# Issuing one transposing load of x from ScalarE, and the first weights all from SyncE

## The chip, the cores and the metric

The kernel runs on one core of one Trainium2 chip. The metric is the device time of one execution in microseconds (us), as the median of several runs. Beside the times there is one profiled execution: a trace with the start and duration of every instruction on every engine, and of the DMA transfers. TensorE is called PE in it (its weight loads PEld), VectorE DVE, ScalarE ACT, GpSimd POOL, SyncE SP. "SPq" and "ACTq" are the instructions of SP and ACT that issue a DMA; the 16 DMA engines of the core then move the data.

## What is computed

Two attention blocks, A and B, of the same shape, with a cache of keys and values; their outputs stand side by side. Each has its own x, k_cache, v_cache, wq and wo, all in bf16.

```python
# B, Sq, D = 16, 32, 1024;  Hq, Hkv, Sk, Dh = 32, 4, 512, 128
q = (x @ wq).reshape(B, Sq, Hq, Dh).transpose(0, 2, 1, 3)
k = jnp.repeat(k_cache, Hq // Hkv, axis=1)
v = jnp.repeat(v_cache, Hq // Hkv, axis=1)
p = softmax(einsum("bhqd,bhkd->bhqk", q, k) * Dh ** -0.5)
o = einsum("bhqk,bhkd->bhqd", p, v)
out = o.transpose(0, 2, 1, 3).reshape(B, Sq, Hq * Dh) @ wo
```

So the work for a block is a projection of 512 tokens by 1024 columns to 32 heads, the attention, and a projection back.

## The kernel before

The bulk of the kernel is one hand-ordered stream of matmuls. A loop of slots (line 613) goes over 128 pairs of a batch entry and a group of heads. In each slot PE gets four score matmuls (line 357), four value matmuls (line 425), and about seven matmuls from a stream of "units" that fill it up: the query projection of the heads still to come (line 301) and the output projections (line 320). Nothing reorders the instructions: each engine runs its own in the order in which the code emits them, and waits on semaphores where data of another engine or of a DMA is needed. DMA issues are instructions in that order too, so a DMA issue that has to wait holds up everything behind it on the same engine.

The change is in the start of the kernel, before that loop (lines 455 to 556). Here the first eight heads of block A are projected. The contraction over the 1024 columns of x goes in eight chunks of 128, called chunk 0 to 7. A matmul of chunk d and head h takes the weights `w0[d // 4][:, d % 4, h]` and the transposed x `xT[0][:, d, :]`, with 512 tokens as columns, and adds into the bank of head h. For each chunk, two things must be on the chip:

- The weights. `load_w0(d0, d1, h0, h1, eng)` loads the rows of chunks d0 to d1 for heads h0 to h1, 32 KB for a chunk and a head. Chunk 0 is loaded in two halves of three heads (96 KB each), chunks 1, 2 and 3 for six heads each (192 KB), the other two heads of chunks 0 to 3 in one transfer (256 KB), then chunk 4, chunks 5 and 6, chunk 7 for all eight heads (256 KB a chunk). In the trace these tiles are called `w_sb`, line 474.
- The transposed x. Chunks 0 and 1 are loaded as they are, in two halves of the tokens (`load_x`, line 465, 128 KB each, one half by SP and one by ACT), transposed by PE (line 521) and copied to `xT` by DVE and ACT (line 525). Chunks 2 and 3, 4 and 5, 6 and 7 are loaded by a DMA that transposes, two chunks at a time (`load_x_transposed`, line 468, 256 KB each).

PE's order there: 22 matmuls on a constant tile (`warm_up`, line 513) while the first data come; the eight transposes of x; chunk 0 of heads 0 to 2 in two halves of the tokens and of heads 3 to 5; chunks 1, 2 and 3 of heads 0 to 5; chunks 0 to 3 of heads 6 and 7; chunks 4, 5 and 6 of all heads; chunk 7 with the copy of each head to `qT` (line 553). All these matmuls have line 531. Behind them come 16 units of line 301 for heads 8 and 9, then the loop.

Order of the DMA issues before the change (SP, if nothing else is named): the second half of x by ACT; the first half of x; chunk 0 of heads 0 to 2; chunk 0 of heads 3 to 5 by ACT; chunk 1; chunk 2 by ACT; the transposing load of chunks 2 and 3; chunk 3; heads 6 and 7 of chunks 0 to 3; chunk 4; the transposing load of chunks 4 and 5; the weights of chunks 5 and 6; the transposing load of chunks 6 and 7; the weights of chunk 7. Then the weights of heads 8 to 11 in two halves (`wq_sb`, line 246), the four transposing loads of the first keys (`kT`, line 275), the weights of heads 12 to 15, the next keys, the first values (`v_sb`, line 283), and so on. ACT loads its table of functions (line 480) between its first two issues.

The DMAs of SP and ACT take their completion semaphores in turn from a set of eight, in the order of the code. An issue whose semaphore was used before waits until the DMA that used it last has completed. Before the change the transposing load of chunks 4 and 5 waits in this way for the load of chunk 0 (heads 0 to 2).

Of the kernel before, what the change touches and what calls it, by code (L numbers as in the profile page):

```python
# [181 lines left out]
def kernel(  # L182
# [14 lines left out]
    nc = tc.nc  # L197
# [20 lines left out]
    def fast_path(ok_i):  # L218
        with ExitStack() as fctx:
# [235 lines left out]
            NF = REP - 2  # L455
# [8 lines left out]
            def load_x(t0, t1, eng=nc.sync):  # L464
                eng.dma_start(out=x_sb[:, t0:t1, :], in_=x_v[:, t0:t1, 0:2 * P])  # L465

            def load_x_transposed(d0):
                nc.sync.dma_start_transpose(
                    out=xT[0][:, d0:d0 + 2, :],
                    in_=A_x.flatten_outer_dims()[:, d0 * P:(d0 + 2) * P],  # L470
                )

            def load_w0(d0, d1, h0, h1, eng=nc.sync):
                eng.dma_start(  # L474
                    out=w0[d0 // HC][:, d0 % HC:(d1 - 1) % HC + 1, h0 * DH:h1 * DH],
                    in_=wq_v[:, d0:d1, h0 * DH:h1 * DH],
                )

            load_x(TT // 2, TT, nc.scalar)
            nc.scalar.preload_act_table_set("natural_log_exp_and_others")  # L480
            load_x(0, TT // 2)
            load_w0(0, 1, 0, NF // 2)
            load_w0(0, 1, NF // 2, NF, nc.scalar)
            load_w0(1, 2, 0, NF)
            load_w0(2, 3, 0, NF, nc.scalar)
            load_x_transposed(2)
            load_w0(3, 4, 0, NF)
            load_w0(0, HC, NF, REP)
            load_w0(HC, HC + 1, 0, REP)
            load_x_transposed(HC)  # L490
            load_w0(HC + 1, DC - 1, 0, REP)
            load_x_transposed(HC + 2)
            load_w0(DC - 1, DC, 0, REP)
            load_wq(0, 2, 0, 2)
# [173 lines left out]
    ok_i = flag.tile([1, 1], I32, name="ok_i")  # L668
    total = 2 * 2 * NG * QW
    ok = fast_path(ok_i)  # L670
    with tc.If(ok < total, preferred_fallthrough_block=True, label="general"):
        general_path(tc, problems, out_flat)
# [30 lines left out]
```

## Time and profile before

| | |
|---|---|
| median of 4 runs | 343.18 us (342.87 to 343.43) |
| the profiled execution | 343.06 us |
| its span, first to last instruction | 341.2 us |
| PE busy | 337.0 us, 99% of the span |
| DVE, ACT, POOL busy | 265.4, 185.4, 47.0 us |
| DMA moved in the span | 71.70 MB, 210 GB/s on average |
| queue of SP and queue of ACT: packets | 127504 and 704 |
| granted clock of PE | 1.0 throughout |

The landing times of the first transfers, by their issues:

| transfer | issued at, by | lands after |
|---|---|---|
| x, first half | 0.74 us, SP | 2.2 us |
| x, second half | 0.82, ACT | 2.6 |
| chunk 0, heads 0 to 2 | 1.25, SP | 2.9 |
| chunk 0, heads 3 to 5 | 1.34, ACT | 3.3 |
| chunk 1 | 1.75, SP | 4.5 |
| chunk 2 | 1.83, ACT | 4.7 |
| chunks 2 and 3 of x, transposing | 2.22, SP | 5.2 |
| chunk 3 | 3.60, SP | 4.3 |
| heads 6, 7 of chunks 0 to 3 | 4.22, SP | 4.6 |
| chunk 4 | 4.69, SP | 5.0 |
| chunks 4 and 5 of x, transposing | 5.25, SP | 5.3 |

How to read it: times in the trace count from the first instruction. A line of a timeline gives start, duration, engine, line of the code, operation, the tile written and the tiles read, and how many instructions were merged into it; in brackets the idle time of that engine before it and what ended it. The chain of waits is followed back from the last instruction: at each step to what released it. The busy share of a DMA queue adds up the durations of its packets, so it can exceed 1 where an engine has packets of two queues under way.

### The profile page before, as it was taken

How to read it: one execution, taken by the hardware profiler on the slowest of the kernel's cores; microseconds unless marked ns; L12 is line 12 of the kernel's file. 1: busy time of each engine (PE TensorE's matmuls, PEld its weight loads, DVE VectorE, ACT ScalarE, POOL GpSimd, SP SyncE). 2: the span in 40 equal slices, each digit the busy share in tenths (PEclk: the TensorE clock that was granted, in tenths of full speed). 3: DMA queues.
4: the chain of work that ended last, by engine and by line, in shares of the span. 5: the costliest groups of instructions: out<-in, count | busy, mean ns of one | idle time of the engine just before them, and what ended most of it. 6: DMA issues, size and time to landing. Idle time of an engine off the chain costs nothing.

```text
span 341.2 us, 5475 instructions
## 1 busy us (share of the span) xinstructions
PE 337.0 (99%) x2113; PEld 213.2 (62%) x2113; DVE 265.4 (78%) x335; ACT 185.4 (54%) x208; POOL 47.0 (14%) x206
## 2 busy tenths in 40 slices
PE   8999999999999999999999999999999999999996
PEld 6455666666666666666666666666666666666555
DVE  0047988888988898888888988879888888889540
ACT  2058666666667667666645545555554555555110
POOL 0001110011111111110012221222122101111100
PEclk9999999999999999999999999999999999999999
DMA  8979999989999898999999965998449997440001
GB/s 200 307 186 263 291 243 222 186 226 267 308 282 154 239 223 234 205 294 303 319 294 273 254 125 146 335 284 224 111 110 292 357 188 177 98 108 12 17 19 33
DMA packets 128622, 71.70 MB, mean 210 GB/s; under 512 B 76880, under 2 KB 127824, under 8 KB 128592
## 3 DMA queue, kind: packets, MB, share of 16 engines
q1 hardware_dynamic: 127504, 69.78, 84.2%
q0 software_dynamic: 384, 1.05, 0.8%
q10 hardware_dynamic: 704, 0.49, 0.5%
q8 instruction: 17, 0.28, 0.4%
q14 instruction: 13, 0.11, 0.1%
HBM read 50.59 MB, written 2.10 MB: 154 GB/s over the span
## 4 chain that ended last, share of the span: by engine, by line
PE 97%; DMA 1%; SPq 0%; ACT 0%; issue 0%; ACTq 0%
PE f_ps L320 32%; PE q_ps L301 28%; PE s_ps L357 16%; PE ob L425 16%; PE q_ps L531 4%; DMA w_sb<-in_A_wq_dram 1%; SPq L465 0%; SPq L474 0%; ACT o_sb L329 0%; ACTq L329 0%
## 5 line engine op out<-in xcount | busy, mean ns | idle before, releaser
L365 ACT ACTIVATE p_sb<-s_ps,shift 128x1024 bf16<-128x1024 f32 x128 | 142.7, 1115 | 97.5 <-PE s_ps L357 87.0
L376 DVE TRANSPOSE_TENSOR_REDUCE parts<-p_sb 128x32 f32<-128x1024 bf16 x128 | 158.8, 1240 | 20.7 <-ACT p_sb L365 19.3
L320 PE MATMUL f_ps<-wo_sb,oT 128*128 128x512 bf16 (+1 forms) x544 | 132.3, 366 | 0.0
L301 PE MATMUL q_ps<-xT,wq_sb 128*128 128x512 bf16 x448 | 116.9, 379 | 0.0
L357 PE MATMUL s_ps<-qT,kT 128*128 128x256 bf16 x512 | 76.8, 273 | 0.0
L425 PE MATMUL ob<-p_sb,v_sb 128*128 128x256 bf16 x512 | 76.8, 273 | 0.0
L320 PEld LDWEIGHTS <-oT 128*128 128x128 bf16 x544 | 53.2, 98 | 35.3
L357 PEld LDWEIGHTS <-kT 128*128 128x128 bf16 x512 | 56.9, 113 | 28.3
L301 PEld LDWEIGHTS <-wq_sb 128*128 128x128 bf16 x448 | 43.8, 98 | 32.2
L425 PEld LDWEIGHTS <-v_sb 128*128 128x128 bf16 x512 | 50.1, 98 | 20.0
L447 DVE TENSOR_TENSOR oT<-r,ob 128x512 bf16<-128x512 f32 x64 | 43.9, 686 | 19.8 <-PE ob L425 19.4
L411 DVE STREAM_TRANSPOSE r<-rall 128x512 f32<-128x512 f32 x64 | 44.2, 691 | 1.1
L309 ACT CAST qT<-q_ps 128x512 bf16<-128x512 f32 x56 | 32.7, 583 | 16.5 <-PE q_ps L301 16.5
L394 POOL COPY half<-cs 64x32 f32<-64x32 f32 x32 | 6.6, 206 | 231.5 <-DVE cs L384 231.5
L329 ACT CAST o_sb<-f_ps 128x512 bf16<-128x512 f32 (+1 forms) x17 | 9.5, 559 | 23.6 <-PE f_ps L320 23.6
L531 PE MATMUL q_ps<-xT,w_sb 128*128 128x512 bf16 (+1 forms) x67 | 14.6, 379 | 0.2 <-DMA w_sb<-in_A_wq_dram 0.2
L406 DVE RECIPROCAL rall<-sums 128x32 f32<-128x32 f32 x32 | 10.5, 327 | 3.3 <-POOL sums L403 3.3
L384 DVE TENSOR_REDUCE cs<-parts 128x32 f32<-128x128 f32 x32 | 12.1, 377 | 1.1
L553 DVE CAST qT<-q_ps 128x512 bf16<-128x512 f32 x4 | 2.5, 682 | 13.3 <-PE q_ps L531 13.3
L531 PEld LDWEIGHTS <-w_sb 128*128 128x128 bf16 x67 | 6.6, 101 | 7.9 <-DMA w_sb<-in_A_wq_dram 0.9
L553 ACT CAST qT<-q_ps 128x512 bf16<-128x512 f32 x4 | 2.1, 599 | 12.8 <-PE q_ps L531 12.8
L331 POOL DMA_DIRECT2D out_dram<-o_sb x8 | 4.6, 575 | 29.2 <-ACT o_sb L329 29.2
(25 smaller groups left out, 48.7 us busy)
## 6 DMA issues: line engine op xcount, KB each, us to landing
v_sb<-in_A_v_cache_dram SPq DMA_DIRECT2D x16, 512.0 KB, 5.9
wq_sb<-in_B_wq_dram SPq DMA_DIRECT2D x8, 1024.0 KB, 5.8
wo_sb<-in_A_wo_dram SPq DMA_DIRECT2D x8, 1024.0 KB, 7.5
v_sb<-in_B_v_cache_dram SPq DMA_DIRECT2D x16, 512.0 KB, 5.2
wo_sb<-in_B_wo_dram SPq DMA_DIRECT2D x8, 1024.0 KB, 8.5
wq_sb<-in_A_wq_dram SPq DMA_DIRECT2D x5, 1024.0 KB, 6.6
wq_sb<-in_A_wq_dram SPq DMA_DIRECT2D x2, 512.0 KB, 7.2
kT<-in_A_k_cache_dram SPq DMA_TRANSPOSE x64, 4.4
```

Source lines behind the costliest of these rows:

```text
L301: nc.tensor.matmul(ps[:], lhsT=w[:, dc, (h % 4) * DH:(h % 4 + 1) * DH], rhs=xT[pr][:, dc, :], start=(dc == 0), stop=(dc == DC - 1),)
L309: nc.scalar.copy(out=qT[pr, g][:, :, hl, :], in_=ps[:].rearrange("p (b s) -> p b s", s=SQ),)
L320: nc.tensor.matmul(ps[:, 0:width], lhsT=oT[pr, tt][:, h, :], rhs=wo_tiles[pr, nh, h // REP][:, h % REP, off:off + width], start=(h == 0), ...
L357: nc.tensor.matmul(s_ps[:, c, :], lhsT=kT[:, i % GRP, c, :], rhs=qT[pr, g][:, b, :, :].rearrange("p h s -> p (h s)"), start=True, stop=True,)
L365: nc.scalar.activation(out=p_sb[:], in_=s_ps[:], func=ACTF.Exp, bias=shift[:], scale=SCALE)
L376: nc.vector.tensor_reduce(out=parts[k][:, q, :, :].rearrange("p c h -> p (c h)"), in_=st[i]["p"][:].rearrange("p c (h s) -> p (c h) s", s=SQ),
L384: nc.vector.tensor_reduce(out=cs[:], in_=parts.pop(k)[:].rearrange("p q c h -> p q h c"), axis=AX.X, op=ALU.add,)
L406: nc.vector.reciprocal(out=rall[:, k, :], in_=quad.pop(k)[:])
L411: nc.vector.transpose(out=r[:].rearrange("p n s -> p (n s)"), in_=rall[:, k, o * 2 * REP:(o + 1) * 2 * REP] .unsqueeze(2).to_broadcast([P, ...
L425: nc.tensor.matmul(ob[j][:, q, :], lhsT=v_sb[:, i % GRP, c, :], rhs=st[i]["p"][:, c, :], start=(c == 0), stop=(c == KC - 1),)
L447: nc.vector.tensor_tensor(out=out, in0=rcp.pop(j)[:].rearrange("p (q h) s -> p q h s", h=REP), in1=ob.pop(j)[:].rearrange("p q (h s) -> p ...
L531: nc.tensor.matmul(first_q[h][:, ts], lhsT=w0[dc // HC][:, dc % HC, h * DH:(h + 1) * DH], rhs=xT[0][:, dc, ts], start=(dc == 0 and t0 == 0 ...
```

## The change

The transposing load of chunks 2 and 3 of x is issued by ACT, after its half of x and its table load, and stands in the code ahead of all weights. The second half of chunk 0 and chunk 2 of the weights, which ACT issued, are issued by SP, in their old places. The computation is the same, and so are the instructions of PE, DVE and POOL. ACT has one DMA issue fewer, SP one fewer of the transposing kind and two more of the plain kind.

```diff
-            def load_x_transposed(d0):
-                nc.sync.dma_start_transpose(
+            def load_x_transposed(d0, eng=nc.sync):
+                eng.dma_start_transpose(
                     out=xT[0][:, d0:d0 + 2, :],
                     in_=A_x.flatten_outer_dims()[:, d0 * P:(d0 + 2) * P],
                 )
...
             load_x(TT // 2, TT, nc.scalar)
             nc.scalar.preload_act_table_set("natural_log_exp_and_others")
             load_x(0, TT // 2)
+            load_x_transposed(2, nc.scalar)
             load_w0(0, 1, 0, NF // 2)
-            load_w0(0, 1, NF // 2, NF, nc.scalar)
+            load_w0(0, 1, NF // 2, NF)
             load_w0(1, 2, 0, NF)
-            load_w0(2, 3, 0, NF, nc.scalar)
-            load_x_transposed(2)
+            load_w0(2, 3, 0, NF)
             load_w0(3, 4, 0, NF)
             load_w0(0, HC, NF, REP)
             load_w0(HC, HC + 1, 0, REP)
```

Since the order in the code has changed, so has the turn of the eight semaphores: in the built kernel the transposing load of chunks 4 and 5 on SP now waits for the completion of the transposing load of chunks 2 and 3 on ACT, and the ones behind it each for one of the loads of chunks 0 to 2. From the first `kT` on the waits are the same as before.

## Prediction

> **What bounds the kernel now.** I read the page's chain first: PE holds 97% of it and DMA 1%, so a transfer can set the time only where PE waits for it. Two pieces of the chain, in its order of time, show the one place:
>
> ```profile
> 1.75 4.53 DMA w_sb<-in_A_wq_dram
> 6.32 12.69 PE q_ps L531 x58
> ```
>
> The weights of chunk 1 (call them w1, and so on by chunk; w0a and w0b are the two halves of chunk 0) are issued at 1.75 us, land at 6.28, and release PE at 6.32. From there to the last matmul I find no gap in PE's instructions. So the change can act in two ways alone: it moves that 6.32, or it makes a new gap behind it. The timeline of PE, columns start, duration, instructions:
>
> ```profile
> 3.24 1.06 PE L521 MATMUL xT_ps<-ident,x_sb 128*128 128x128 bf16 x8
> 4.21 1.92 PE L531 MATMUL q_ps<-xT,w_sb 128*128 128x256 bf16 x9
> 6.32 12.69 PE L531 MATMUL q_ps<-xT,w_sb 128*128 128x512 bf16 x58 [0.19 <-DMA w_sb<-in_A_wq_dram]
> 18.85 3.62 PE L301 MATMUL q_ps<-xT,wq_sb 128*128 128x512 bf16 x16
> ```
>
> 58 matmuls start in 18.85 - 6.32 = 12.53 us: 0.216 us each. The ninth of the group before starts at 5.75, so PE would be free for w1 at 5.96. The bubble is 6.32 - 5.96 = 0.36 us, and that is all a faster start can win, but for some 0.1 us if w0a, which lands at 4.17 just ahead of the 4.21, came sooner. Then the queues, SP's and ACT's timelines:
>
> ```profile
> 0.74 0.45 SPq L465 DMA_DIRECT2D x_sb<-in_A_x_dram  x1
> 1.25 0.92 SPq L474 DMA_DIRECT2D w_sb<-in_A_wq_dram  x2
> 2.22 1.33 SPq L468 DMA_TRANSPOSE xT<-in_A_x_dram  x1
> 3.60 1.60 SPq L474 DMA_DIRECT2D w_sb<-in_A_wq_dram  x3
> 5.25 1.60 SPq L468 DMA_TRANSPOSE xT<-in_A_x_dram  x1
> 6.89 0.58 SPq L474 DMA_DIRECT2D w_sb<-in_A_wq_dram  x1
> 1.34 0.94 ACTq L474 DMA_DIRECT2D w_sb<-in_A_wq_dram  x2
> 3.91 0.80 ACT L525 COPY xT<-xT_ps 128x256 bf16<-128x256 bf16 x2 [1.31 <-PE xT_ps L521]
> ```
>
> The first transposing load (chunks 2 and 3, called T2; T4 and T6 follow) costs its queue 1.33 us to issue and lands 5.2 us after 2.22, at 7.43. PE wants it with chunk 2, six matmuls after 6.32, at 7.63: 0.2 us to spare. Last, the DMA engines by windows; the last two columns are their busy share and GB/s:
>
> ```profile
> 1.00:2.00 1.00, 1.00 (x11) 1.00 (x12) 0.00 (x0) 0.69 (x1) 0.32 (x2) 1.00 0.07 21
> 2.00:3.00 1.00, 1.00 (x12) 1.00 (x11) 0.00 (x0) 0.60 (x1) 0.00 (x0) 1.00 0.91 274
> 3.00:4.00 1.00, 1.00 (x13) 1.00 (x10) 0.29 (x1) 0.09 (x1) 0.00 (x0) 1.00 0.88 218
> 4.00:5.00 1.00, 1.00 (x7) 0.62 (x6) 0.29 (x1) 0.66 (x2) 0.00 (x0) 1.00 0.98 281
> 5.00:6.00 1.00, 1.00 (x7) 0.45 (x4) 0.00 (x0) 0.00 (x0) 0.00 (x0) 1.00 1.24 177
> 6.00:7.00 1.00, 0.81 (x5) 0.33 (x5) 0.00 (x0) 0.00 (x0) 0.00 (x0) 1.00 1.10 271
> 7.00:8.00 1.00, 1.00 (x6) 0.47 (x5) 0.00 (x0) 0.00 (x0) 0.00 (x0) 1.00 1.11 289
> ```
>
> They are busy from 2 us on, so bytes and their order set the landings, not the moment of issue. Two facts from the records of single packets. First, while both queues hold weights, an engine takes one packet of SP's and one of ACT's in turn; where T2 meets leftover weights the same is seen (weight packets starting at 5.526, 5.602, 5.677 us: one 61 ns weight packet and one 14 ns packet of T2 per turn). Second, T2 stops at its half: 13 packets started between 5.39 and 5.92 take 240 to 768 ns instead of 18, and all end near 6.15, when the last engine is through its weights. That is the 177 GB/s row.
>
> **The change, part by part.**
>
> *Issue.* T2 leaves SP (1.33 us) for ACT, at 1.34, where w0b and w2 were (0.45 us each). SP issues x, w0a, w0b, w1, w2, w3, the last two heads of chunks 0 to 3 (w0-3), and w4 in a row, about 0.5 us each: w0b at 1.75, w1 at 2.25, w3 at 3.25, w4 at 4.3. ACT's queue is done with T2 at 1.34 + 1.33 = 2.67, at worst 1.34 + 3.51 = 4.85 (the longest transposing issue in the trace, L275 at 11.92). Behind it stand the two copies of L525, now at 3.91, for chunk 1, which PE starts at 5.96: even 4.85 + 0.80 is in time. Cost nothing.
>
> *w0b* now lands behind x (256 KB), w0a and itself (192) and its share of T2 (16 of 64 packets an engine, 64 KB). Before, it landed at 4.64 with the first two alone, so 64 KB / 245 GB/s later (245 is 1,047 KB by 6.28, summed over the windows, in the 4.28 us from 2.0): 4.9. PE wants it at 5.32. Hidden.
>
> *w1.* Before: x 256, w0a and w0b 192, w1 and w2 in turn 384, together 832 KB to 6.28. With turns against T2: 256 + 192 + 192 + 24/64 of T2 (96) = 736 KB, 96 KB less, 0.39 us sooner: 5.9. If T2 were served whole ahead of it: 896 KB, 6.28 + 0.26 = 6.54. I take about 6.0, being nearer to the turns that the packets show: gain 0.3 us. Chunk 2 is then wanted at 6.0 + 6 x 0.216 = 7.3.
>
> *T2.* This is the term that decides. T2 has 64 packets an engine. In turns it ends beside w0a, w0b, w1, w2, w3 (8 each) and 24 of w0-3's 32: 256 + 768 + 192 + 256 = 1,472 KB. Before, its last packet left at 6.85 after 1,201 KB by the windows. 271 KB more at the 289 GB/s of the 7 to 8 row is 0.93 us: 7.78, and with the 0.58 from last packet to landing 8.36. Against that, in the 177 GB/s stretch the held engines had nothing else to move; now SP's queue has w3 and w0-3 for them. Regained: about 281 - 177 = 100 KB, 0.35 us, so 8.0. If instead T2 gets more packets a turn it ends with w2, at 1,088 KB, and lands at 7.0. The bounds are 7.0 and, with the hold felt twice (8.36 plus up to 0.75), 9.1. I take 8.0. Chunk 2 starts at 8.05, against 7.63: a loss of 0.42, the 0.3 of w1 swallowed in it.
>
> The Trainium skill speaks against the change here: "DMA: Bandwidth & Descriptors", section "Issuing engines are not separate DMA queues", says that DMAs from several engines share the same 16 DMA engines and interleave, and that issuing from more of them saves only the issue time. By that rule alone T2's landing would stay put and the sum would be the w1 term at most; the packets' turns agree with the interleaving and add that T2 loses its place.
>
> *SP behind T2.* T4's issue waits on the semaphore that T2 completes (the eight DMA semaphores go round, and T2 and T4 now share one), so at 5.25 before, at 8.0 now. That is new, and SP's queue is behind it. T4: 8.0 + 3.3 (a transposing load half its size took 2.65, L275 at 18.87, plus half of T2's 1.15 us of packets) = 11.3; at the worst 8.0 + 5.3 = 13.3, its landing time under a full queue, which there will hardly be. PE wants chunk 4 after 20 more matmuls: 8.05 + 4.31 = 12.36. Chunks 5 to 7 keep a similar margin. The DMA engines run dry for about 0.3 us before T4 and 0.6 us behind it, so what follows slides by about 1 us: the first wq_sb (lands 16.7, wanted at 18.85) and the kT of slot 0 (19.2, wanted 22.3) have more; the wq_sb for head 12 (issued 20.17, lands 25.86, wanted 27.07) has 1.2, and 1.6 once PE itself is 0.42 later. Cost nothing; without that cover, whatever exceeds 1.6 us.
>
> *Sum.* Profiled execution: 343.06 us, of which 341.2 is the span and 1.86 lies around it. 343.06 + 0.42 = 343.5. The median of the runs shown is 343.18, 0.12 above it, so 343.6.
>
> **Rivals.**
>
> *A: T2 is much later (slower).* Place: the matmuls of chunk 2. If a held transposing packet also blocks the weights behind it on its engine, nothing is regained: 8.36, plus the hold itself. It decides once T2 lands after 8.32, where the loss is 0.69. Price: 8.36 to 9.1, 0.8 to 1.5 us, typically 344.2. For: the DMA share of 1.24 beside 177 GB/s shows packets that occupy engines without moving bytes. Against: the slow engines, which set the end, are not themselves held.
>
> *B: T2 goes ahead in larger portions, or fills the pauses in the weights.* It lands by 7.3 and w1 gates alone, between 5.96 and 6.54: -0.36 to +0.22, about 343.0. For: the 13 held packets started after long unbroken runs of T2. Against: the turns of one.
>
> *C: the slide on SP comes out at PE.* T2 lands late and the 1 us grows past 1.6 us, at head 12 or the first kT: another 0.5 to 1, 344.5. For: SP is in order and its kT issues already took 8.21 us. Against: they were held by full queues, which give the delay back.
>
> *D: it does nothing.* SP stalls on T2 all the same and the bytes are the same: 343.2 within 0.1. That is the middle of B and is counted there.
>
> **How the numbers follow.** Forecast 0.40, A 0.27, B with D 0.27, C 0.06. What a measurement of this kernel can tell from no change is about 0.2%, 0.69 us. The forecast's own range is 343.3 to 343.87 and lies within it; a win above 0.69 exceeds the whole bubble, so faster gets 0.03; A and C make slower 0.32, allowing a little of A to stay under; same 0.65. The range takes in B's gain and most of A: 342.8 to 344.5.
>
> **What would show it.** In the profile after: T2's issue on ACT at about 1.34; w1 landing near 6.0 and chunk 1 starting there; a new gap of about 0.7 us before chunk 2, put down to the transposing load; SP waiting until about 8.0 ahead of T4; no gap at chunks 4 to 7 or at L301. If the gap is before chunk 1 and not before chunk 2, T2 was served first and B holds. If the first gap is after 12 us, C does. If T2 lands beyond 8.4, A. A time under 342.7 would mean that something in the start which I hold fixed, the first 4.2 us, has moved.

## The result, and the profile after

| | before | after |
|---|---|---|
| median | 343.13 us (72 runs, 342.42 to 343.68) | 343.98 us (46 runs, 343.13 to 348.85) |
| after / before | | 1.0044, 95% interval 1.0033 to 1.0056 |
| forecast | | 343.6 (342.8 to 344.5) |

The kernel became slower by 0.44%, beyond what can be told from no change. The ratio is near that of the means (344.80 / 343.09, 1.0050); the medians alone give 1.0025, because the changed kernel has something that the one before has not: executions that differ by 5.7 us among themselves, against 1.3. The profile that came with the result is of an execution at 348.60 us, among the longest. A second profile of the same kernel, run again as the first experiment, is of one at 344.33 and is read first. Both lie above the median: an execution with a smaller loss was not profiled.

PE's timeline in that second profile (start, duration; in brackets the idle time ahead and what ended it):

```profile
4.36 1.40 PE L531 MATMUL q_ps<-xT,w_sb 128*128 128x256 bf16 x6
6.92 13.34 PE L531 MATMUL q_ps<-xT,w_sb 128*128 128x512 bf16 x61 [1.16 <-DMA w_sb<-in_A_wq_dram]
20.10 3.62 PE L301 MATMUL q_ps<-xT,wq_sb 128*128 128x512 bf16 x16
```

Before, nine matmuls ran without a break from 4.21, six for heads 0 to 2 of chunk 0 and three for heads 3 to 5. Now only the first six do. The three for heads 3 to 5 stand at the head of the group that starts at 6.92, behind 1.16 us of idle time. From there no further gap appears up to line 301, which starts at 20.10 instead of 18.85. These 1.25 us are the whole loss of this execution: 344.33 - 343.06 = 1.27.

What was late is in the chain of the same profile:

```profile
1.75 5.13 DMA w_sb<-in_A_wq_dram
6.92 13.12 PE q_ps L531 x60
```

SP's issue at 1.75 is w0b. It landed at 6.88; before, issued by ACT at 1.34, it landed at 4.64. The queues of SP and ACT look as forecast:

```profile
1.25 3.66 SPq L474 DMA_DIRECT2D w_sb<-in_A_wq_dram  x7
7.10 1.34 SPq L468 DMA_TRANSPOSE xT<-in_A_x_dram  x1
```

```profile
1.34 1.33 ACTq L468 DMA_TRANSPOSE xT<-in_A_x_dram  x1
4.13 0.80 ACT L525 COPY xT<-xT_ps 128x256 bf16<-128x256 bf16 x2 [1.53 <-PE xT_ps L521]
```

T2 is issued at 1.34 in 1.33 us, the seven loads of weights in a row from 1.25, and T4 waits for T2's landing at 7.09. The windows of the DMA engines (the last two columns are their busy share and GB/s):

```profile
3.00:4.00 1.00, 0.96 (x11) 0.63 (x9) 0.08 (x1) 0.00 (x0) 0.00 (x0) 1.00 1.16 290
4.00:5.00 1.00, 1.00 (x9) 0.71 (x8) 0.50 (x2) 0.75 (x2) 0.00 (x0) 1.00 1.34 133
5.00:6.00 1.00, 0.76 (x4) 0.27 (x2) 0.00 (x0) 0.00 (x0) 0.00 (x0) 1.00 1.22 181
6.00:7.00 1.00, 0.08 (x1) 0.08 (x2) 0.00 (x0) 0.00 (x0) 0.00 (x0) 1.00 1.01 229
```

From 4 to 5 us, when w0b should come, the engines are busier than in any row shown of before (1.34, against 1.24 at most) and move 133 GB/s; before, the same row had 281. T2 and w0 are under way together there, on two queues, and that is what the row shows: packets that hold engines without moving bytes.

The long execution (348.60 us) has the same gap, longer, and one thing more. PE's timeline, then its windows (behind the window and its length PE's busy share and matmuls; third from the end the granted clock):

```profile
5.27 0.83 PE L531 MATMUL q_ps<-xT,w_sb 128*128 128x256 bf16 x6 [1.13 <-DMA w_sb<-in_A_wq_dram]
8.63 15.89 PE L531 MATMUL q_ps<-xT,w_sb 128*128 128x512 bf16 x61 [2.54 <-DMA w_sb<-in_A_wq_dram]
24.36 1.89 PE L301 MATMUL q_ps<-xT,wq_sb 128*128 128x512 bf16 x8
```

```profile
6.00:7.00 1.00, 0.10 (x1) 0.00 (x0) 0.00 (x0) 0.00 (x0) 0.00 (x0) 1.00 1.16 163
7.00:8.00 1.00, 0.00 (x0) 0.00 (x0) 0.00 (x0) 0.00 (x0) 0.00 (x0) 0.51 1.02 137
8.00:9.00 1.00, 0.36 (x1) 0.13 (x2) 0.00 (x0) 0.00 (x0) 0.00 (x0) 0.50 0.99 285
...
12.00:13.00 1.00, 1.00 (x4) 0.43 (x3) 0.00 (x0) 0.00 (x0) 0.00 (x0) 0.50 0.67 185
13.00:14.00 1.00, 1.00 (x4) 0.33 (x3) 0.00 (x0) 0.00 (x0) 0.00 (x0) 0.58 1.16 277
14.00:15.00 1.00, 1.00 (x6) 0.49 (x5) 0.00 (x0) 0.00 (x0) 0.00 (x0) 1.00 1.23 160
```

w0b lands at 8.59, so PE starts 8.63 - 6.92 = 1.71 us later than in the other profile. But the 61 matmuls behind it also take 15.89 us instead of 13.34: after the idle time the clock was granted at half, from 7.0 to 13.8, with a matmul of 512 columns started every 0.43 us instead of every 0.216 (the counts in the rows include matmuls that reach over an edge of the window). 1.71 + 2.55 is the 4.26 by which line 301 is later.

That the clock has a part in the other long executions too is seen in the mean granted clock, which is on record for each. Of the 46 runs, the 31 below 345.3 us have 0.998 or more. Of the 15 at 345.3 or above, eight have 0.995, about one stretch of 3.4 us at half clock, and two have 0.99, like the profiled one. The other five have 1.0, which a longer wait alone would give, and also a first full grant that comes late (see the last section).

### The profile page after: what moved, and what is told of

Its sections match the earlier page's. It is cut to its first block, busy times and chain, and to the rows that moved or that the text cites. A ratio compares the mean times of both kernels' runs of the same rounds, so it can differ in the third digit from the quotient of the medians.

```text
span 346.7 us, 5475 instructions
## 1 busy us (share of the span) xinstructions
PE 339.0 (98%) x2113; PEld 213.4 (62%) x2113; DVE 265.4 (77%) x335; ACT 185.3 (53%) x208; POOL 47.0 (14%) x206
## 4 chain that ended last, share of the span: by engine, by line
PE 97%; DMA 2%; SPq 0%; ACT 0%; issue 0%; ACTq 0%
PE f_ps L320 32%; PE q_ps L301 28%; PE ob L425 16%; PE s_ps L357 16%; PE q_ps L531 5%; DMA w_sb<-in_A_wq_dram 2%; SPq L465 0%; SPq L474 0%; ACT o_sb L329 0%; ACTq L329 0%
## 5 line engine op out<-in xcount | busy, mean ns | idle before, releaser
L531 PE MATMUL q_ps<-xT,w_sb 128*128 128x512 bf16 (+1 forms) x67 | 16.7, 416 | 3.7 <-DMA w_sb<-in_A_wq_dram 3.7
L406 DVE RECIPROCAL rall<-sums 128x32 f32<-128x32 f32 x32 | 10.4, 326 | 3.3 <-POOL sums L403 3.3
```

The source lines that it names most:

```text
L406: nc.vector.reciprocal(out=rall[:, k, :], in_=quad.pop(k)[:])
L531: nc.tensor.matmul(first_q[h][:, ts], lhsT=w0[dc // HC][:, dc % HC, h * DH:(h + 1) * DH], rhs=xT[0][:, dc, ts], start=(dc == 0 and t0 == 0 ...
```

## The experiments

"Before" in a sentence means the kernel before, in runs on the same chip. The landing times come from the semaphore events of the traces, the counts from the single packets.

**e1_again: the changed kernel once more.**

> The changed kernel once more, for a second profile and for the spread of its time. Both theories: a median near 343.98 us. Theory M (mixing): a transposing load on one queue and copies on the other, on the same DMA engines, hold each other up; each profile then shows the weights of chunk 0 (heads 3 to 5) landing later than 5.3 us, by an amount that differs from one execution to the next, and the transposing load landing at 7.5 us or later. Theory Q (queue order): the weights are late because they all stand in one queue and share the engines with the transposing load in even turns; then their landings repeat to within 0.3 us in every profile.

Measured: 343.73 us (343.28 to 347.78, 11 runs), 1.002 (0.9997 to 1.0044); before 343.35. One run at 347.78, ten from 343.28 to 344.38. Its profile is the one read above. So the mechanism, a late w0b, is there without the long gap, at 1.2 us, and in the profiled long execution it is the same thing made worse. w0b lands 1.71 us apart in the two profiles, as theory M said and theory Q did not; T2's 7.09 is earlier than M's 7.5.

**e2_weights_only: only the weights move to SP.** T2 stays where it was.

```diff
-            load_w0(0, 1, NF // 2, NF, nc.scalar)
+            load_w0(0, 1, NF // 2, NF)
-            load_w0(2, 3, 0, NF, nc.scalar)
+            load_w0(2, 3, 0, NF)
```

> All first weights on SP, but the transposing load of chunks 2 and 3 stays on SP in its old place behind chunk 2's weights. Theory M: no copy runs beside a transposing load on another queue, so no hold: within 0.3 us of the kernel before (342.9 to 343.5) and a spread as small as before's. Theory Q: the weights of chunk 0 (heads 3 to 5) and of chunk 2 still lost ACT's queue: slower by 0.5 us or more.

Measured: 343.68 (343.08 to 344.24), 1.0012 (1.0003 to 1.0021). w0b lands at 4.58 and w1 at 5.59: with the weights alone on one queue they come sooner than before. The profile has two small gaps instead, for T2 and for w3:

```profile
4.09 3.02 PE L531 MATMUL q_ps<-xT,w_sb 128*128 128x256 bf16 x15
7.33 1.46 PE L531 MATMUL q_ps<-xT,w_sb 128*128 128x512 bf16 x6 [0.22 <-DMA xT<-in_A_x_dram]
8.95 10.10 PE L531 MATMUL q_ps<-xT,w_sb 128*128 128x512 bf16 x46 [0.16 <-DMA w_sb<-in_A_wq_dram]
```

So this half of the change makes no late w0b and no long executions. The loss, 0.33 us, lies between the two theories.

**e3_sp_first: T2 ahead of the weights, all on SP.** The order of the changed kernel without the second queue.

```diff
+            load_x_transposed(2)
             load_w0(0, 1, 0, NF // 2)
-            load_w0(0, 1, NF // 2, NF, nc.scalar)
+            load_w0(0, 1, NF // 2, NF)
             load_w0(1, 2, 0, NF)
-            load_w0(2, 3, 0, NF, nc.scalar)
-            load_x_transposed(2)
+            load_w0(2, 3, 0, NF)
```

> The same order of issues as in the changed kernel, but the transposing load stands on SP ahead of all weights, so it runs in one queue with them. Theory M: it lands near 5 us, unmixed; chunk 1's weights come behind 896 KB and land near 6.6, chunk 0's near 5.5: slower than before by 0.2 to 0.8 us with a small spread. Theory Q: as slow as the changed kernel or slower, since the weights stand behind all of it.

Measured: 344.06 (343.49 to 345.6), 1.0031 (1.0017 to 1.0044). T2 lands at 4.90, w0a at 5.27, w0b at 5.80, w1 at 6.92:

```profile
5.32 1.48 PE L531 MATMUL q_ps<-xT,w_sb 128*128 128x256 bf16 x9 [0.82 <-DMA w_sb<-in_A_wq_dram]
6.97 12.69 PE L531 MATMUL q_ps<-xT,w_sb 128*128 128x512 bf16 x58 [0.17 <-DMA w_sb<-in_A_wq_dram]
```

Two things follow. T2 ahead of the weights costs by its place alone, here 0.64 us at line 301 (19.49). And with no weights beside it on the other queue (only the last 51 packets of x) T2's 1,024 packets leave in 1.2 us (3.12 to 4.31), where before they took 2.1. The spread was not small, as theory M had it: four of the 11 runs lie at 344.97 to 345.6, and why was not seen.

**e4_t2_only: only T2 moves to ACT.** w0b and w2 stay on ACT, behind it.

```diff
+            load_x_transposed(2, nc.scalar)
             load_w0(0, 1, 0, NF // 2)
...
-            load_x_transposed(2)
```

> Only the transposing load moves to ACT, ahead of ACT's two weight loads, which stay on ACT as in the kernel before. Theory M: SP's weights of chunk 0 (heads 0 to 2) and chunk 1 still run beside it: as slow as the changed kernel, or slower as ACT's weights of chunk 0 (heads 3 to 5) wait behind it, with a wide spread (above 2 us). Theory Q: two queues for the weights again: near the kernel before, within 0.4 us.

Measured: 346.98 (346.08 to 348.88, 5 runs), 1.0094 (1.0078 to 1.0109). w0b is now behind T2 in the same queue, and T2 lies beside SP's weights: T2 lands at 8.65, w0b at 9.38.

```profile
9.43 15.51 PE L531 MATMUL q_ps<-xT,w_sb 128*128 128x512 bf16 x61 [2.93 <-DMA w_sb<-in_A_wq_dram]
```

The 61 matmuls take 15.51 us, so this is half clock again. Moving the weights to SP therefore saved most of what moving T2 would have cost.

**e5_filler: the gap filled with work.** The changed kernel, with 20 matmuls on the constant tile between heads 0 to 2 and heads 3 to 5 of chunk 0.

```diff
+            warm_up(20)
             first_heads(range(NF // 2, NF), (0,))
```

> The changed kernel with 20 more matmuls of 128 columns on the constant tile, put on PE between chunk 0 of heads 0 to 2 and chunk 0 of heads 3 to 5, where PE waits 1.2 to 2.8 us for weights. They keep PE busy for 1.1 to 2.1 us and compute nothing that is used. Theory C (clock): the executions of the changed kernel at 346 to 349 us pay twice, for the wait and because PE idles so long that its clock is granted at half for about 6.8 us afterwards, which costs some 3 us; with the filler PE does not idle long, and no execution is above 345.5. Rival: the slow executions are slow because the weights land 3 to 5 us later; then the filler changes nothing and about a third of the executions stay above 345.5.

Measured: 344.01 (343.38 to 345.98, 12 runs), 1.0028 (1.0013 to 1.0043). One run of 12 lies above 345.5, where none was expected; of the 57 of the changed kernel so far, 16 lie at 345.3 or above. None of the 12 has a lowered mean clock. This points to PE's idle time as the cause of the long executions, but with 12 runs it isn't conclusive.

**e6_plain: a plain load on ACT instead of a transposing one.** As e2, and ACT issues a plain load of the same 256 KB of x, into room that nothing reads, where the changed kernel has T2.

```diff
+            nc.scalar.dma_start(out=x_sb[:, :, 2 * P:4 * P], in_=x_v[:, :, 2 * P:4 * P])
             load_w0(0, 1, 0, NF // 2)
```

> Like e2 (all first weights on SP, the transposing load in its old place on SP), and ACT also issues a plain load of the same 256 KB of x, where the changed kernel has its transposing load, into an unused part of x_sb. Theory M (only a transposing load mixed with copies holds them up): 256 KB more to move costs up to 0.9 us at 290 GB/s, the weights of chunk 0 (heads 3 to 5) land by 5.4 us and the spread stays below 1.5 us: 343.5 to 344.3. Rival (any load on ACT beside the weights on SP does it): those weights land after 6 us, and the time is as wide as the changed kernel's or wider, above 345 in a third of the executions.

Measured: 343.93 (343.45 to 344.64, 12 runs), 1.0024 (1.0015 to 1.0033). w0b lands at 5.20, and no run is long. The same bytes on the same queue at the same place make w0b 0.6 us later than in e2, not 2.3 as in e1: it is the transposing kind of load that does the rest.

**e7_mirror: the queues exchanged.** T2 on SP behind x, both halves of chunk 0 on ACT, the other weights on SP behind T2.

```diff
-            load_w0(0, 1, 0, NF // 2)
+            load_x_transposed(2)
+            load_w0(0, 1, 0, NF // 2, nc.scalar)
             load_w0(0, 1, NF // 2, NF, nc.scalar)
...
-            load_w0(2, 3, 0, NF, nc.scalar)
-            load_x_transposed(2)
+            load_w0(2, 3, 0, NF)
```

> The two queues exchanged: the transposing load on SP right behind SP's half of x, the two halves of chunk 0's weights on ACT beside it. Theory M: mixing is the same from the other side: chunk 0's weights for heads 3 to 5 land later than 6 us, median above 343.8 and a spread above 2 us. Rival (ACT's queue is the slow place for a transposing load): it is then on SP, so like e3: a transposing load that lands near 5 us and weights of chunk 0 that land by 5.3, with 343.3 to 344.0 as chunk 0 is not behind it.

Measured: 343.47 (343.0 to 343.8, 11 runs), 1.0007 (0.9998 to 1.0016). The times that I expected of the mixture did not come: no long run, and a loss that can't be told. What it does to the transfers stood: w0b lands at 6.09, T2 at 6.20, and their last packets leave together (5.23 and 5.07).

```profile
4.11 0.83 PE L531 MATMUL q_ps<-xT,w_sb 128*128 128x256 bf16 x6
6.14 13.34 PE L531 MATMUL q_ps<-xT,w_sb 128*128 128x512 bf16 x60 [1.20 <-DMA w_sb<-in_A_wq_dram]
```

The gap is there as in e1, but 0.8 us sooner, since T2 is through sooner.

**e8_w2_on_sp: only w2 moves to SP.**

```diff
-            load_w0(2, 3, 0, NF, nc.scalar)
+            load_w0(2, 3, 0, NF)
```

> A version that might beat both: as the kernel before, but chunk 2's weights go on SP behind chunk 1's, so that the two no longer take turns; the weights of chunk 0 (heads 3 to 5) stay on ACT and the transposing load stays on SP. In e2 chunk 1's weights landed at 5.59 us instead of 6.28. Expected: PE starts chunk 1 without a wait at 5.96 and gains up to 0.36 us, if the transposing load still lands by 7.3: 342.8 to 343.1. Rival: the transposing load, or chunk 3's weights, land later and take the gain: 343.2 to 343.6, as in e2.

Measured: 343.27 (342.73 to 343.56, 11 runs), 1.0002 (0.9993 to 1.001). w1 lands at 5.11 instead of 6.28, and the bubble of 0.36 us is gone from the profile; line 301 starts at 18.68, only 0.17 sooner, since w0a landed at 4.56 and PE began chunk 0 later, at 4.61. The time does not show it. That bubble was nearly all that a faster start could win.

**e9_swapped: only chunk 0 on SP.** T2 on ACT as in the change, with w1 and all later weights up to chunk 4 behind it on ACT (the copies of chunk 1 of x then on DVE).

```diff
+            load_x_transposed(2, nc.scalar)
             load_w0(0, 1, 0, NF // 2)
...
-            load_w0(1, 2, 0, NF)
+            load_w0(1, 2, 0, NF, nc.scalar)
...
-            load_w0(HC, HC + 1, 0, REP)
+            load_w0(HC, HC + 1, 0, REP, nc.scalar)
```

> e7 with the two queues exchanged again: the transposing load on ACT as in the changed kernel, but only the two halves of chunk 0's weights stand on SP beside it; the weights of chunks 1 to 4 and of heads 6 and 7 follow behind it on ACT. DVE makes the copies of chunk 1 of x that ACT made. Theory D (dose): the hold grows with the copies that run beside the transposing load, so with 192 KB of them it is as mild as e7: median 343.2 to 343.9, no execution above 344.8. Rival (a transposing load issued by ACT is the slow one): as the changed kernel, with about a third of the executions above 345.

Measured: 344.38 (343.81 to 346.21, 10 runs), 1.0038 (1.0022 to 1.0054). With only 192 KB of copies on the other queue, w0b still lands with T2, 6.45 and 6.69. And the same pairing appears a second time, T4 on SP beside chunk 4 on ACT. The chain:

```profile
1.35 5.34 DMA xT<-in_A_x_dram
6.69 0.02 issue
6.71 6.66 DMA xT<-in_A_x_dram
```

T4 takes 6.66 us to land; in e1, with no copies on the other queue, it took 3.9. PE waits for it at chunk 4, until 13.41. Theory D failed (the median is above 343.9, two runs are above 344.8), but with this second wait in the time the rival isn't shown either.

**e10_idle and e11_idle_filled: idle time by itself.** The kernel before, with three fills of a large tile on DVE ahead of the second half's copies, so that PE stands idle at a known place with no DMA late. In e11 30 matmuls on the constant tile fill that time.

```diff
             for k, ts in enumerate(((0, TT // 2), (TT // 2, TT))):
+                if k:
+                    for _ in range(3):
+                        nc.vector.memset(rall[:], 1.0)
```

What e11 adds to this:

```diff
+            first_heads(range(0, NF // 2), (0,), 0, TT // 2)
+            warm_up(30)
+            first_heads(range(0, NF // 2), (0,), TT // 2, TT)
```

> The kernel before, with its DMAs unchanged, but three writes of 128x1024 numbers on DVE hold back the copy of the second half of chunk 0 of x by about 3 us, so that PE idles from about 4.9 to 7.6 us; the values written are replaced later. It measures the idle time by itself. Rival (idle time costs its length): PE starts again some 2.7 us late and regains the 0.36 us bubble: about 345.5, all executions within 1 us. Theory C (clock): in some or all executions the clock of PE is granted at half for 3.4 or 6.8 us after the gap, which adds 1.7 to 3.4 us: executions at 347 to 349.

> e10 with 30 matmuls on the constant tile in the gap (1.6 us at the full clock, 3.2 at half), which compute nothing that is used. Theory C: PE's clock is kept or comes back sooner, and the time falls to about 345.5 in nearly all executions, below e10 by 1.5 us or more. Rival: the same as e10 or later by what the filler runs over.

Measured: 347.31 (347.13 to 348.26, 4 runs), 1.0127 (1.0112 to 1.0141), against 346.05 (345.24 to 347.2, 6 runs), 1.0087 (1.0068 to 1.0105). PE's timeline of e10, then of e11:

```profile
7.85 15.34 PE L531 MATMUL q_ps<-xT,w_sb 128*128 128x256 bf16 x64 [2.82 <-DVE xT L525]
23.03 3.19 PE L301 MATMUL q_ps<-xT,wq_sb 128*128 128x512 bf16 x14
```

```profile
7.97 13.65 PE L531 MATMUL q_ps<-xT,w_sb 128*128 128x256 bf16 x64
21.46 3.62 PE L301 MATMUL q_ps<-xT,wq_sb 128*128 128x512 bf16 x16
```

Both resume within 0.12 us of each other; after the idle time the same 64 matmuls take 1.69 us more. In e10 the clock is recorded at half from 8.18 to 11.59, 3.41 us, which costs half of itself. So idle time of this length is followed by half clock, apart from any DMA. Of e11's six runs three lie at 345.24 to 345.57, as theory C said, and three at 346.53 to 347.2; those weren't profiled.

**e12_mirror_all: T2 on SP, chunks 0 to 3 of the weights all on ACT.** Added lines, against the changed kernel:

```diff
+            load_x_transposed(2)
+            load_w0(0, 1, 0, NF // 2, nc.scalar)
             load_w0(0, 1, NF // 2, NF, nc.scalar)
+            load_w0(1, 2, 0, NF, nc.scalar)
...
+            load_w0(3, 4, 0, NF, nc.scalar)
+            load_w0(0, HC, NF, REP, nc.scalar)
```

> The changed kernel with its two queues exchanged: the transposing load of chunks 2 and 3 on SP right behind SP's half of x, and on ACT beside it the weights of chunks 0 to 3 and of heads 6 and 7, in the changed kernel's order; chunk 4's weights stay on SP behind the transposing load. DVE makes the copies of chunk 1 of x that ACT made. With e7 (SP, only chunk 0's weights beside it), e9 (ACT, only chunk 0's) and the changed kernel (ACT, all) it completes a table of four. Theory D (dose): with all weights beside it the transposing load is slow from either queue: median above 343.7, some of the executions above 345. Theory S (side): issued by SP it is served fast, lands by 6.3 us as in e7, and no execution is above 344.5. Both: the last weights of chunk 0 land within 0.5 us of the transposing load, because it is served ahead of them.

Measured: 345.87 (345.83 to 347.19, 5 runs), 1.0085 (1.0072 to 1.0099). w0b and T2 again land together, 7.12 and 7.36, close to the 6.88 and 7.09 of e1. So theory S failed: issued by SP, T2 is no faster beside the same first weights, and a T2 on ACT isn't needed for the late w0b.

```profile
7.17 16.07 PE L531 MATMUL q_ps<-xT,w_sb 128*128 128x512 bf16 x60 [0.72 <-DMA w_sb<-in_A_wq_dram]
```

PE ran at half clock up to 12.7, and no further gap follows. The times are no clean test of the side, since ACT's issue of w3 now waits for T2: w3 lands at 11.76, ahead of its use only because PE was at half clock, and it may cost in other executions.

**e13_behind_w0b: the changed kernel, w0b back on ACT ahead of T2.** If a late w0b were all, this should mend it.

```diff
+            load_w0(0, 1, NF // 2, NF, nc.scalar)
             load_x_transposed(2, nc.scalar)
             load_w0(0, 1, 0, NF // 2)
-            load_w0(0, 1, NF // 2, NF)
```

> The changed kernel with one thing undone: the weights of chunk 0 for heads 3 to 5 go back to ACT, ahead of the transposing load, which stays on ACT behind them; all other weights on SP. Theory W (the late weights of chunk 0, and the clock that PE loses while it waits for them, are the cost; the transposing load is served ahead of whatever copies stand beside it): these weights land by 5.2 us, the hold passes to chunk 1's weights, which land with the transposing load near 7 us, PE idles about 1 us there and keeps its clock: median 343.6 to 344.3 and no execution above 345. Rival (the forecast's mechanism, equal turns): chunk 1's weights land near 6.0, the transposing load last, and chunk 2 waits for it.

**e14_act_in_place: only the queue of T2 changes.** The kernel before, T2 in its place in the code, but issued by ACT.

```diff
-            load_x_transposed(2)
+            load_x_transposed(2, nc.scalar)
```

> The kernel before, with the transposing load of chunks 2 and 3 issued by ACT instead of SP, behind ACT's weights of chunks 0 and 2; nothing else is moved. It waits there until ACT's half of x has landed (3.45 us in the kernel before). Theory W: chunk 0's and chunk 1's weights are ahead of it and land as before (4.6 and 6.3 us), the copies held beside it are those of chunk 3 and of heads 6 and 7, which PE wants after 8.9 us; only its own landing counts, at 7.4 to 8.3 us: 343.2 to 344.0 and no execution above 345. Rival (a transposing load on the other queue costs as in the changed kernel, wherever it stands): median above 343.7 and a spread above 2.5 us.

Measured: e13 346.35 (345.05 to 346.67, 6 runs), 1.0086 (1.0071 to 1.01); e14 346.40 (345.7 to 346.7, 5 runs), 1.0089 (1.0076 to 1.0102). Both are worse than the change. In e13 w0b is on time (4.45), and T2 is the one that is late; from its chain and its timeline:

```profile
1.83 8.53 DMA xT<-in_A_x_dram
```

```profile
10.40 6.20 PE L531 MATMUL q_ps<-xT,w_sb 128*128 128x512 bf16 x27 [1.85 <-DMA xT<-in_A_x_dram]
16.89 5.35 PE L531 MATMUL q_ps<-xT,w_sb 128*128 128x512 bf16 x24 [0.29 <-DMA w_sb<-in_A_wq_dram]
```

In e14 T2 lands as late, at 10.29 us, and w1 is late too:

```profile
7.37 1.47 PE L531 MATMUL q_ps<-xT,w_sb 128*128 128x512 bf16 x6 [0.61 <-DMA w_sb<-in_A_wq_dram]
10.33 6.20 PE L531 MATMUL q_ps<-xT,w_sb 128*128 128x512 bf16 x27 [1.49 <-DMA xT<-in_A_x_dram]
16.92 5.35 PE L531 MATMUL q_ps<-xT,w_sb 128*128 128x512 bf16 x24 [0.38 <-DMA w_sb<-in_A_wq_dram]
```

T2 is not late for the same reason in the two. In e13 its packets start at 4.18 and take 5.4 us. In e14 they start only at 7.00, when w2 ahead of them in ACT's queue is through, against 4.81 before; this later start is 2.2 of the 2.9 us by which T2 lands later. Both make chunk 2 wait for T2, which the forecast expected of the change and which the change did not show. And the last row of each is the slide on SP: T4 was held until T2 had landed, at 10.3, and chunk 5's weights behind it came 0.3 to 0.4 us too late. e13 and e14 refute theory W, by which only w0b is at stake: in e13, saving it moves the loss to T2.

All together, T2 by kernel (us):

```
                   T2's packets    T2       w0b      copies on the other
                   first to last   landed   landed   queue beside T2
e3_sp_first         3.12 -  4.31    4.90     5.80    none (the end of x)
before              4.81 -  6.87    7.43     4.64    the rest of w2
e5_filler           3.33 -  5.27    6.44     6.16    all weights, from w0a
e1_again            3.32 -  6.07    7.09     6.88    all weights, from w0a
after               3.14 -  7.80    8.80     8.59    all weights, from w0a
e7_mirror (on SP)   3.11 -  5.07    6.20     6.09    w0a, w0b
e9_swapped          3.28 -  5.59    6.69     6.45    w0a, w0b
e12_mirror_all (SP) 3.26 -  6.29    7.36     7.12    w0a to w2
e4_t2_only          3.25 -  7.37    8.65     9.38    w0a, w1, w3 and later
e13_behind_w0b      4.18 -  9.55   10.36     4.45    w1 and later weights
e14_act_in_place    7.00 -  9.84   10.29     4.42    w3 and later weights
```

## Why the prediction was wrong

The median of 343.98 us lies near the forecast's 343.6, but the gap that the forecast priced did not come and another did, so that this nearness is luck.

**The start that could be won.** Right: the bubble of 0.36 us was about the ceiling. e8 removes it and gains nothing that can be measured.

**Issue.** Right. T2 took 1.33 us on ACT, the weights about 0.5 us each on SP, and the copies of line 525 were in time. The bound of 3.51 us as the longest transposing issue was misread: line 277 has one of 7.98 us in the trace before. Nothing came of it.

**w0b, "lands at 4.9, hidden".** This step failed. It gave T2 a share of 64 KB while w0b was under way, by turns of one packet each. In e1 between 3.5 and 6.0 us T2 gave 936 packets and chunk 0's weights 146, some six to one, and w0b's last packet left with T2's (6.18 and 6.07). So w0b did not land 0.26 us later but 2.24 later, or 3.95 in the long execution. The term that was put at nothing was the loss: 1.16 us of idle time in e1 and 2.54 in the other, which also waited 1.13 us for w0a. The turns of one had been read from three packets of the trace before. A count over a stretch was to be had there too: from 5.0 to 6.0 us, T2 gave 441 packets while the last 42 of w1 and w2 went. It would have been a warning, not a proof, since engines that had no weights left may have served T2 alone. The hold at T2's half was miscounted as well: 16 packets, not 13, start between 5.39 and 5.92, take 240 to 768 ns and end near 6.15.

The Trainium skill, "DMA: Bandwidth & Descriptors", section "Queues, rings and completion order", says that a DMA engine serves the queues in turn, but drains a whole packet, typically 9 to 17 descriptors and at most 64, before it switches. T2 has 64 records on each engine, so if the trace's records are those descriptors, the rule allows T2 several records a turn, at the most all of them. That fits the six to one better than turns of one; no run here shows where such a packet ends.

**w1, "about 6.0".** Not reached: 7.43 in e1. But chunk 1 was by then held by w0b, and no gap stands ahead of it.

**T2, "8.0, and chunk 2 waits 0.42".** T2 landed at 7.09 in e1 and at 8.80 in the long execution. With PE later, chunk 2 was wanted at 6.92 + 9 x 0.216 = 8.86, so the gap did not come. As a mechanism it exists: in e13 and e14, other orders of issue, T2 at 10.3 to 10.4 makes chunk 2 wait 1.5 to 1.9 us, beyond the upper bound of 9.1.

**SP behind T2.** Right for this change. T4 was issued at 7.10, or 8.81 in the long execution, and no gap follows at chunks 4 to 7. The cover is smaller than the forecast said: with T4 held until 10.3, in e13 and e14, 0.3 to 0.4 us came out at PE.

**The rivals.** B had the mechanism, T2 ahead in larger portions, but priced only w1 behind it and so came to 343.0; w0b stands in the same queue ahead of w1. A had the direction and the size, at the wrong place.

**The clock.** The forecast took the clock as 1.0 throughout and priced a wait as its length alone. In the long execution 2.55 of the 4.26 us by which it is behind e1 are the clock's, and a window of 3.41 us that PE works through at half costs 1.7 (e10). It is the long executions that carry the ratio from 1.0025, by the medians, to 1.0044; ten of the 15 in the 46 runs have a lowered mean clock. How much of each is the clock and how much the transfer was seen in the profiled one alone.

What stays open: why T2 beside the same copies takes 1.9 us of packets in one execution (e5) and 4.6 in another (after), where from 3.5 to 5.0 us T2 gave 61 to 74 packets each half microsecond and chunk 0's weights 6 to 40; and whether the engine that issues T2 matters a little, since e7 and e9 (6.20 and 6.69) and e12 and e1 (7.36 and 7.09) differ either way and each is one profile. With T2 on ACT, a T4 on SP that doesn't wait for it wasn't tried: the skill's same page, section "Silent corruption: two transposing streams in flight at once", requires the later stream to wait for the earlier one's full completion, and no run here tests it.

## What to carry to other kernels

A queue of its own is not a lane of its own: before moving a transposing load to another queue, list the copies that will then be under way beside it and look which of them the path waits for first. Keep what is needed first out of that company, by landing it before the transposing load starts, and let the transposing load follow in the same queue, as the kernel before did, which no version here beat. Read the service of two queues from counts over the whole transfer, not from a few packets that alternate, and where a new wait leaves PE idle, add the clock's part to the price.

## What the runs showed of the hardware

**A transposing load and copies slow each other.** T2 alone (e3) is through in 1.2 us. Beside copies of another queue it took 1.9 to 5.4 (e5, e13), and the copies waited as well: in e13 the weights of chunks 1 to 3, which land by 5.59, 6.09 and 8.90 in e2, land at 7.04, 9.37 and 10.72. Moving only T2's issue from SP to ACT, in place (e14), costs 3.1 us; there most of T2's delay is its later start behind w2, not the mixing. A plain load of the same bytes in T2's place (e6) delays w0b by 0.6 us, T2 by 2.3 (e1).

**The clock is granted in windows of 3.41 us.** The two stretches at half clock in the midst of the work are 3.41 us long (e10) and 6.83 (the long execution); the stretches at full clock, 334.51 (e10) and 337.92 (e1), are 98 and 99 times 3.413. The idle time lies ahead of the half clock: in e10 PE was idle from 5.03 to 7.85, and the half clock ran from 8.18 to 11.59, while PE was busy. Where the windows fall differs by execution: the first full grant came at 3.60 in the long execution, at 5.16 in the kernel before, at 5.57 in e1. A gap of 1.16 us (e1) or 1.85 (e13) cost nothing more than itself, with full clock afterwards; gaps of 2.82 (e10) and 2.54 (the long execution) were followed by one window and two at half. In e4 and e12 the first full grant itself came only at 13.85 and 12.72; their gaps fell into the windows before it, which may be why. The column of the granted clock starts with the first full grant and reads 1.00 before, so there only the spacing of the matmuls shows it: 512 columns every 0.43 us in e4 up to 13.67, every 0.216 later. In the kernel before it is the same up to 5.16, where matmuls of 256 columns start every 0.21 us and then 0.11 apart; its "1.0 throughout" holds from there on.

The Trainium skill, "TensorE: Matmul & The Clock Gate", section "What's actually happening", gives the window as free-running and 3413 ns long; the records agree with the length. It gives an idle window as the condition for the drop. Here none was idle throughout: in the long execution the window from 3.60 to 7.01 held about 1.4 us of work and the next was at half clock, so less than an idle window was enough. In e13 the window from 6.89 to 10.30 held about 1.6 us, and the clock stayed full. Where the edge lies, these runs don't settle.
